# Output projection and second LayerNorm of an attention chunk ranked above older feed-forward work, in a one-core transformer block

## The chip, the cores and the metric

The kernel runs on one core of one Trainium2 chip. The metric is device time in microseconds (us), lower is better. A profile of one execution comes with each kernel; its span, from first to last instruction, is about 2 us shorter than the device time. Engines are named as the profile names them: PE is TensorE (matmul), PEld its weight loads, ACT is ScalarE, DVE is VectorE, POOL is GpSimd, SP issues the DMAs. L1039 is line 1039 of the kernel. Matmuls overlap in the records, so the cost of a matmul in a row is taken from the distance of their starts, not from the mean duration of one.

## The reference

A pre-LayerNorm transformer block: 2048 tokens, width 640, 32 heads of 20 columns, gated feed-forward (GLU) of width 1728, bf16.

```python
h  = x + attention(layernorm(x)) @ wo            # softmax over 2048 keys, 32 heads
hn = layernorm(h)                                # "LN2"
g  = hn @ w_gate ; u = hn @ w_up                 # 640 -> 1728
out = h + (gelu(g) * u) @ w_down                 # 1728 -> 640
```

## The kernel before

The queries are cut into seven chunks, numbered 0 to 6. The softmax needs 2048 x 2048 exps per head; ACT computes most of them, DVE eight tiles per slot (two in the first) with a polynomial; a slot is one chunk with a group of its heads. While ACT works on one chunk, PE fills the time between score and attention matmuls with work of earlier chunks: output projection, LN2, gate, up and down projection.

No engine program is written by hand. Every operation is recorded with a priority, and a list scheduler in the kernel's Python picks, for each engine, the ready operation with the lowest priority number, and the lowest recording number among equals (on PE an operation of the kind that ran last may go first). Its result is a fixed order of instructions per engine, with semaphore waits between them.

```python
SIZES = (512, 512, 256, 256, 256, 128, 128)
D_PER_SLOT = (8, 8, 8, 8, 8, 8, 8)               # exp tiles on DVE in each slot, per chunk
P_QK, P_PV, P_PRO, P_EPI, P_BG = 0, 1, 1.5, 2, 3
```

Two parts of one function record what follows the attention of a chunk. `tail` is true for chunk 6 only.

```python
def post(c, banks, tail):                        # cut
    p = P_EPI if tail else P_BG
    for tt in range(tb, tb + nt):
        # transpose of the attention output: by DMA, in the tail by PE and an ACT copy
        for hf in range(2):                      # output projection, 5 matmuls per half (L616)
            list(chain(bk, key, 320, [...wo...], [("hnT", tt), "wo"], p))
            op("dve", ...h_sb += bank..., p, ..., rel=[bk])                     # L1007
        ln_stats(h_sb[:, tt, :], t, ..., p)
    ln_rsqrt(q0 // 128, nt, p, table=tail)       # in the tail: Sqrt on ACT
    # normalize, transpose ...
    p = P_BG
    for k in range(nb):                          # gate (L1039), copied out by DVE (L1074)
        bg, kg = mms(k, wg, "wg", ...)
        cp.append(op("dve", ...tensor_copy..., p, ...))
    gl.append(op("act", ...Gelu..., -1, mode="gelu", ..., after=cp))
    for k in range(nb):                          # up (L1039), multiply by DVE (L1085)
        bu, ku = mms(k, wu, "wu", ...)
        hdone.append(op("dve", ...ALU.mult..., p, ...))
    # down (L1096), residual add (L1100), output DMA
```

A gelu needs another activation table than exp, so a gelu block in the exp phase has a table load before and one after it (1.28 us each in the traces). The scheduler also puts in filler matmuls, which compute nothing, where PE would otherwise have too little to do.

## Time and profile before

| | |
|---|---|
| device time, three runs | median 928.82 us (928.81 to 929.91) |
| span of the profiled run | 927.4 us |
| first steady exp, near 92 us, to the end of the last exp | 92.91 to 890.21: 797.3 us |
| the tail: end of the last exp to the end of the span | 37.2 us |

I call the second line the exp phase. It starts at the exp that waits 0.57 us for PE near 92 us.

From the page: part 1 (busy time, share of the span, instructions), and the shares by engine of the chain of work that ended last.

```profile
PE 837.1 (90%) x10069; PEld 356.9 (38%) x10126; DVE 811.3 (87%) x1703; ACT 883.2 (95%) x799; POOL 39.1 (4%) x117
ACT 73%; PE 14%; DVE 9%; DMA 2%; POOL 1%; issue 1%; SPq 0%
```

ACT sets the pace for most of the span. The tail is different. The timeline of ACT from 886 us (start, duration, what; in brackets how long ACT was idle before, and what ended it):

```profile
888.62 1.59 ACT L339 ACTIVATE rege<-ps 128x1536 bf16<-128x1536 f32 x1
890.23 1.28 ACT L339 ACT_TABLE_LOAD   x1
...
896.02 0.70 ACT L567 ACTIVATE rege<-ps 128x640 bf16<-128x640 bf16 x1 [4.29 <-PE ps L561]
901.39 0.21 ACT L339 ACTIVATE sd<-sd 128x1 bf16<-128x1 bf16 x1 [4.67 <-DVE sd L339]
901.61 1.28 ACT L339 ACT_TABLE_LOAD   x1
...
903.60 0.70 ACT L567 ACTIVATE rege<-ps 128x640 bf16<-128x640 bf16 x1 [0.49 <-PE ps L561]
904.20 1.69 ACT L339 ACTIVATE rege<-rege 128x1792 bf16<-128x1792 bf16 x1
```

These are: the last exp, the load for Sqrt, the copy of the last attention transpose, the Sqrt of the last LN2, the load for gelu, the copy of the last LN2's transpose, and last the gelu of chunk 5. The timeline of PE, without the small attention matmuls:

```profile
888.39 3.57 PE L1096 MATMUL ps<-regw,rege 128*128 128x320 bf16 x25
...
896.90 1.52 PE L616 MATMUL ps<-wo,rege 128*128 128x320 bf16 x10
898.26 0.98 PE L1096 MATMUL ps<-regw,rege 128*128 128x320 bf16 x6
899.08 4.21 PE L1039 MATMUL ps<-rege,regw 128*128 128x128 bf16 x70
903.12 0.44 PE L561 MATMUL ps<-ident,xn_t 128*128 128x128 bf16 x5
904.36 6.54 PE L1039 MATMUL ps<-rege,regw 128*128 128x128 bf16 x114 [0.80 <-ACT rege L567]
...
920.58 3.98 PE L1096 MATMUL ps<-regw,rege 128*128 128x320 bf16 x28 [0.52 <-DVE rege L1064]
```

PE hardly rests: it is idle 0.80 us before the 114 matmuls and 0.52 us before the last down projection. What it works on, above all, is the down projection of chunk 4 and the whole GLU of chunk 5, left over from the exp phase.

### The profile page before, as it was taken

Reading aid. Unit: us, or ns where it says so; the run is one execution under the profiler, and the core shown is the slowest. Engines: PE = TensorE matmul, PEld = TensorE weight load, DVE = VectorE, ACT = ScalarE, POOL = GpSimd, SP = SyncE. Lnnn points to the kernel's source line nnn. Section 1 sums busy time; section 2 is a strip of 40 time slices with the busy share of each in tenths; the row PEclk is TensorE's granted clock in tenths of the full one; section 3 lists DMA queues with packets and bytes.
Section 4 is the critical chain, followed back from the end, with each engine's and each line's share of the span. In section 5 each row is a group of like instructions: output and inputs, shape, how many; then the busy total and the mean of one; then the engine's idle time right before and its main releaser. Section 6 shows DMA issues by size and latency. Waiting matters only on the chain.

```text
span 927.4 us, 23141 instructions
## 1 busy us (share of the span) xinstructions
PE 837.1 (90%) x10069; PEld 356.9 (38%) x10126; DVE 811.3 (87%) x1703; ACT 883.2 (95%) x799; POOL 39.1 (4%) x117
## 2 busy tenths in 40 slices
PE   3998999899998998998797898999899998989998
PEld 2432322222232222233233333344345455546677
DVE  8859999999898998888798997988998997899972
ACT  6899999999999999999999999999999999999951
POOL 5000000000001000000001000000200200010100
PEclk9999999999999999999999999999999999999999
DMA  7301010322540000001021000011000100101000
GB/s 256 94 19 43 18 55 18 90 60 66 155 176 18 12 1 1 1 15 44 1 31 23 8 2 1 16 30 31 16 16 2 23 23 2 31 17 24 3 24 16
DMA packets 39517, 34.36 MB, mean 37 GB/s; under 512 B 19436, under 2 KB 36936, under 8 KB 39416
## 3 DMA queue, kind: packets, MB, share of 16 engines
q1 hardware_dynamic: 39416, 32.89, 12.7%
q8 instruction: 79, 1.29, 0.6%
q14 instruction: 22, 0.18, 0.1%
HBM read 20.12 MB, written 8.09 MB: 30 GB/s over the span
## 4 chain that ended last, share of the span: by engine, by line
ACT 73%; PE 14%; DVE 9%; DMA 2%; POOL 1%; issue 1%; SPq 0%
ACT pts L339 46%; ACT rege L339 25%; PE ps L1039 3%; PE ps L616 3%; DVE qt_all L339 3%; PE ps L1096 3%; PE ps L852 3%; PE ps L339 2%; DVE rege L339 2%; DMA regw<-in_A_wqkv_dram 1%; ACT L339 1%; DVE rege L812 1%; DVE qt_all L812 1%; POOL nw L339 0%; PE ps L561 0%
## 5 line engine op out<-in xcount | busy, mean ns | idle before, releaser
L339 ACT ACTIVATE pts<-ps 128x1536 bf16<-128x1536 f32 x480 | 571.7, 1368 | 5.1 <-PE ps L852 3.8
L852 PE MATMUL ps<-qt_all,kt_all 32*128 32x256 bf16 (+2 forms) x3584 | 304.9, 289 | 51.2 <-ACT pts L339 29.1
L339 ACT ACTIVATE rege<-ps 128x1536 bf16<-128x1536 f32 x239 | 298.8, 1367 | 2.4 <-PE ps L339 1.5
L852 PEld LDWEIGHTS ps<-qt_all,kt_all 32*128 32x128 bf16 x3584 | 96.4, 92 | 279.8 <-ACT pts L339 160.0
L339 DVE TENSOR_TENSOR qt_all<-qt_all 128x1024 bf16<-128x1024 bf16 (+1 forms) x240 | 164.4, 685 | 3.7
L1039 PE MATMUL ps<-rege,regw 128*128 128x256 bf16 (+2 forms) x957 | 149.2, 287 | 10.3 <-ACT rege L339 2.8
L339 PE MATMUL ps<-pts,v_all 128*21 128x256 bf16 (+2 forms) x2098 | 138.8, 290 | 1.0 <-DVE rege L339 1.0
L812 DVE TENSOR_SCALAR rege<-ps 128x512 int16<-128x512 f32 x154 | 105.3, 684 | 23.9 <-PE ps L852 23.1
L339 DVE TENSOR_SCALAR qt_all<-qt_all 128x1024 bf16<-128x1024 int16 (+1 forms) x288 | 115.8, 417 | 2.4
L339 PE MATMUL ps<-rege,v_all 128*21 128x256 bf16 (+2 forms) x1294 | 113.3, 292 | 0.1
L1039 PEld LDWEIGHTS ps<-rege,regw 128*128 128x128 bf16 x980 | 72.0, 97 | 65.4 <-issue 27.3
L616 PE MATMUL ps<-regw 128*128 128x512 bf16 (+1 forms) x342 | 82.1, 349 | 3.8 <-issue 1.3
L1096 PE MATMUL ps<-regw,rege 128*128 128x320 bf16 x448 | 78.7, 301 | 1.1 <-DVE rege L1064 0.5
L812 DVE TENSOR_SCALAR qt_all<-ps 128x512 int16<-128x512 f32 x96 | 65.6, 684 | 4.5 <-PE ps L852 3.6
L339 DVE TENSOR_SCALAR rege<-rege 128x1024 int16<-128x1024 int16 (+2 forms) x166 | 67.2, 421 | 1.3
L339 DVE TENSOR_TENSOR rege<-rege 128x1024 bf16<-128x1024 bf16 (+3 forms) x103 | 65.5, 644 | 0.9
L339 PEld LDWEIGHTS ps<-pts,v_all 128*21 128x21 bf16 x2098 | 50.2, 91 | 37.9 <-issue 31.7
L339 PE MATMUL ps<-kt_all,zer 128*32 128x512 bf16 x680 | 56.4, 384 | 0.0
L1085 DVE TENSOR_TENSOR rege<-rege,ps 128x512 bf16<-128x512 bf16 (+1 forms) x53 | 35.8, 677 | 16.4 <-PE ps L1039 16.4
L1096 PEld LDWEIGHTS ps<-regw,rege 128*128 128x128 bf16 x448 | 37.0, 97 | 32.7 <-issue 15.6
L339 PEld LDWEIGHTS ps<-rege,v_all 128*21 128x21 bf16 x1294 | 41.0, 91 | 20.6 <-issue 13.6
L616 PEld LDWEIGHTS ps<-regw 128*128 128x128 bf16 x360 | 28.6, 98 | 45.3 <-issue 20.9
(95 smaller groups left out, 575.3 us busy)
## 6 DMA issues: line engine op xcount, KB each, us to landing
rege<-in_A_x_dram SPq DMA_DIRECT2D x6, 640.0 KB, 5.2
q_rows<-regw SPq DMA_DIRECT2D x20, 128.0 KB, 1.7
out_dram<-rege SPq DMA_DIRECT2D x16, 160.0 KB, 2.0
regw<-in_B_w_gate_dram SPq DMA_DIRECT2D x1, 2160.0 KB, 13.3
regw<-in_B_w_up_dram SPq DMA_DIRECT2D x1, 2160.0 KB, 18.3
regw<-in_B_w_down_dram SPq DMA_DIRECT2D x1, 2080.0 KB, 23.4
kt_all<-k_rows SPq DMA_DIRECT2D x12, 160.0 KB
qt_all<-q_rows SPq DMA_DIRECT2D x12, 160.0 KB
```

The source lines that it names most:

```text
L339: return lambda eng: getattr(eng, method)(*args, **kwargs)
L616: yield op("pe", lambda eng, l=l, r=r, k=k: eng.matmul(bank(bk, n), l, r, start=(k == 0), stop=(k == len(steps) - 1)), c_mm(n), prio, mode ...
L812: d_ops.append(op("dve", lambda eng: eng.tensor_scalar(v[:, 512 * h:512 * h + 512], bank(b), EXP_MUL, -32000.0, ALU.mult, ALU.max), c_dve( ...
L852: return lambda eng: eng.matmul(out()[:, kk * nq:(kk + 1) * nq], kt_all[32 * j:32 * j + 32, g, kt * 128:(kt + 1) * 128], qt_all[32 * j:32 ...
L1039: op("pe", lambda eng, a=a, f=f, fi=fi: eng.matmul(bank(bk)[:, fi * nq:(fi + 1) * nq], w[:, a, F0[f]:F0[f] + 128], hnT[:, a, 128 * tb:128 ...
L1085: hdone.append(op("dve", lambda eng, bu=bu, fv=fv, w=w: eng.tensor_tensor(fv, fv, bank(bu, w), ALU.mult), c_dve(w), p, reads=[ku] + hkeys( ...
L1096: op("pe", lambda eng, f=f, o=o, hf=hf, bk=bk: eng.matmul(bank(bk, 320), ha_f[:, o:o + 128], wd[:, f, hf * 320:(hf + 1) * 320], start=(f = ...
```

## The change

The intent: a chunk's output projection and LN2 should not queue behind the older GLU matmuls, so that its own GLU can start earlier.

```diff
-D_PER_SLOT = (8, 8, 8, 8, 8, 8, 8)
+D_PER_SLOT = (8,) * len(SIZES)
-P_QK, P_PV, P_PRO, P_EPI, P_BG = 0, 1, 1.5, 2, 3
+P_QK, P_PV, P_PRO, P_EPI, P_LN, P_BG = 0, 1, 1.5, 2, 2.5, 3
@@ def post
-            p = P_EPI if tail else P_BG
+            p = P_EPI if tail else P_LN
-                                   for a in range(NA)], [("hnT", tt), "wo"], p))
+                                   for a in range(NA)], [("hnT", tt), "wo"], p, after=(sc.lw[("h", tt, hf)],)))
```

The first pair is the same tuple: there are seven sizes. The last line makes the output projection wait for the load of the chunk's residual input.

## The prediction

> **What bounds the kernel.** ScalarE, for most of the span: the page gives ACT 883.2 us busy (95%), and busy time by stretches 98 to 100% from 100 to 890 us. The chain of waits is 73% ACT. From 100 to 890 us ACT waits under 3 us in all. PE is near its limit too (95% from 700 to 800 us). After the last exp (890.2 us) the limit changes: the chain of the last 37 us is mostly PE (down projection L1096, gate/up L1039), with PE idle only 0.8 us at 904.4 and 0.5 us at 920.6.
>
> **What the change does.** The tuple for VectorE exp tiles has seven eights, as before: no change, and instruction totals confirm it. What is left is priority: output projection and LN2 ahead of older GLU work. Everything else is only moved, except 17 fewer filler matmuls (13 full, 4 narrow) and two more ACT table loads.
>
> **The exp phase.** ACT's work before the last exp is unchanged; the gelu blocks of three chunks move 8 to 12 exps earlier. I expect 0 +- 1 us. PE takes the earlier work in place of fillers and idle.
>
> **The tail, from the instruction order.** Now 53 down matmuls of chunk 4 follow the last score matmul; then 24 do. The 29 are worth 29 x 0.136 us (28 take 3.80 us) = 3.9 us of PE work. But chunk 5's gelu then stands between the last attention transpose copy and the Sqrt of the last LN2, with two added loads (1.28 us each). The trace shows 1.30 us from load to next activation; the Trainium skill, "ScalarE: Activation LUTs", section "What ACT_TABLE_LOAD costs", has about 2.66 us with a drain, which this trace does not show. Estimate: the gelu load hides in a wait; gelu starts at about 901.3, when the last gate copy is done; 1.69 us, load 1.28, Sqrt at 904.3 instead of 901.4. PE has no chunk work from about 899.8 to 903.0 (eight fillers and a wait), some 3.2 us. Then chunk 5's up matmuls cover the later LN2: its transposes come at about 905.9 instead of 903.1. At 0.057 us for a 128-column matmul the last up matmul ends at about 919.2 instead of 920.1.
>
> So 3.9 us less PE work, about 3 us more waiting: net -0.9 us. **Predicted 928.0 us** (before 928.82), range 925.8 to 930.3. Chances: faster by over 2% 0.01, within 2% 0.97, slower by over 2% 0.02. Two per cent is 18.6 us, half of the tail.
>
> **What would show it.** Right: the last exp ends at 890 +- 1, ACT over 99% busy to there; in the tail two more table loads around a 1.7 us gelu, the Sqrt about 3 us later, about 3 us of fillers and idle on PE before chunk 5's first up matmul. Wrong: ACT idle well over 3 us between 100 and 890 us; a PE stall on the chunk's residual input, for which the added dependency makes the output projection wait; the end over 2 us earlier, which would mean that the PE wait was smaller than I count.
>
> **What would make it wrong.** PE matmuls run in program order. Moved GLU matmuls that wait for a late VectorE copy (VectorE 88% busy) would hold back score matmuls and starve ACT; each such stall is tenths of a us, so dozens are needed for 2%. Fewer fillers might lower the granted clock; it is 1.0 almost throughout and I expect no change.

## The result

Time after: 927.52 us median of 4 runs (927.23 to 927.85); before, in the same rounds, 929.37 (928.81 to 931.93). The ratio of the fast runs is 0.9975, with a 95% interval of 0.9955 to 0.9994: a little faster. All ratios here are the mean time of one kernel's fast runs over that of the other's of the same rounds, so not quite the ratio of the medians quoted. A repetition later (e10) gave 0.9966 (0.9953 to 0.9980).

The two profiled spans are 927.4 and 925.5 us. They split into three parts:

| us | before | after | difference |
|---|---|---|---|
| up to the first steady exp | 92.91 | 92.84 | -0.07 |
| exp phase | 797.30 | 796.56 | -0.74 |
| tail | 37.19 | 36.10 | -1.09 |

The tail repeats within 0.1 us in every later profile of the two kernels, but the exp phase of the kernel before does not: two later looks at it (e11 and e12) took 798.06 and 798.05 us, while the changed kernel took 796.52 us again (e10). So the exp phase gains 0.7 us against this profile and 1.5 us against the other two. Two waits of ACT in this profile of the kernel before, and one that only the other two looks have (this is e12's), are absent after the change:

```profile
671.25 2.37 ACT L339 ACTIVATE pts<-ps 128x1536 bf16<-128x1536 f32 x2 [0.17 <-PE ps L852]
...
728.76 1.02 ACT L339 ACTIVATE rege<-ps 128x1024 bf16<-128x1024 f32 x1 [0.32 <-PE ps L852]
```

```profile
673.85 2.36 ACT L339 ACTIVATE rege<-ps 128x1536 bf16<-128x1536 f32 x2 [0.33 <-PE ps L852]
```

The same lines of the page, after:

```profile
PE 845.3 (91%) x10109; PEld 354.8 (38%) x10109; DVE 810.3 (88%) x1703; ACT 885.7 (96%) x801; POOL 35.1 (4%) x117
ACT 72%; PE 14%; DVE 11%; issue 1%; POOL 0%; DMA 0%
```

PE's busy time rises by 8.2 us although the program has 17 matmuls fewer. The count of records also rose, by 40, so part of this is only records that were missing in the first trace. The Trainium skill warns of this number in "Trainium Kernel Development and Optimization", section "Performance Expectations": matmul busy time is a bad metric for how close a kernel is to roofline, because matmuls are pipelined. Here it would mislead as a measure of work as well: it rises while the span falls.

ACT in the tail, after, from the last exp on:

```profile
887.77 1.63 ACT L339 ACTIVATE rege<-ps 128x1536 bf16<-128x1536 f32 x1
889.42 1.28 ACT L339 ACT_TABLE_LOAD   x1
...
895.62 0.70 ACT L567 ACTIVATE rege<-ps 128x640 bf16<-128x640 bf16 x1 [4.71 <-PE ps L561]
896.35 1.28 ACT L339 ACT_TABLE_LOAD   x1
900.49 1.70 ACT L339 ACTIVATE rege<-rege 128x1792 bf16<-128x1792 bf16 x1 [2.86 <-DVE rege L1074]
902.21 1.28 ACT L339 ACT_TABLE_LOAD   x1
903.50 0.21 ACT L339 ACTIVATE sd<-sd 128x1 bf16<-128x1 bf16 x1
903.72 1.28 ACT L339 ACT_TABLE_LOAD   x1
...
905.52 0.70 ACT L567 ACTIVATE rege<-ps 128x640 bf16<-128x640 bf16 x1 [0.30 <-PE ps L561]
```

The gelu of chunk 5 (900.49) now stands before the Sqrt (903.50), with a load on each side. PE in the tail, after:

```profile
887.57 3.43 PE L1096 MATMUL ps<-regw,rege 128*128 128x320 bf16 x24
...
896.49 1.52 PE L616 MATMUL ps<-wo,rege 128*128 128x320 bf16 x10
897.85 1.45 PE L1039 MATMUL ps<-rege,regw 128*128 128x128 bf16 x23
900.51 1.90 PE L339 MATMUL ps<-kt_all 128*128 128x512 bf16 x8 [1.21 <-DVE rege L1074]
902.25 2.96 PE L1039 MATMUL ps<-rege,regw 128*128 128x128 bf16 x50
905.04 0.44 PE L561 MATMUL ps<-ident,xn_t 128*128 128x128 bf16 x5
905.32 2.06 PE L1039 MATMUL ps<-rege,regw 128*128 128x128 bf16 x34
...
918.74 3.98 PE L1096 MATMUL ps<-regw,rege 128*128 128x320 bf16 x28 [0.52 <-DVE rege L1064]
```

Before, 53 down matmuls (L1096) of chunk 4 ran after the last score matmul; now 24 do. The 29 that went are worth 29 x 0.136 = 3.9 us. But between the end of the gate matmuls (897.85 + 1.45 = 899.30) and the first up matmul (902.25) PE has 2.95 us without work: 1.21 us idle and eight fillers. So most of the gain was given back. Adding up: -3.94 (down matmuls), +2.95 (this hole), -0.80 (the old wait before the 114, gone), +0.85 (two new waits for gate copies, 0.34 us at 894.02 and 0.51 us at 896.09) is -0.94; measured -1.09, so 0.15 us stays unassigned.

### The profile page after: what moved, and what is told of

Its sections match the earlier page's. It is cut to its first block, busy times and chain, and to the rows that moved or that the text cites. A ratio compares the mean times of both kernels' runs of the same rounds, so it can differ in the third digit from the quotient of the medians.

```text
span 925.5 us, 23154 instructions
## 1 busy us (share of the span) xinstructions
PE 845.3 (91%) x10109; PEld 354.8 (38%) x10109; DVE 810.3 (88%) x1703; ACT 885.7 (96%) x801; POOL 35.1 (4%) x117
## 3 DMA queue, kind: packets, MB, share of 16 engines
q8 instruction: 79, 1.29, 0.6%
## 4 chain that ended last, share of the span: by engine, by line
ACT 72%; PE 14%; DVE 11%; issue 1%; POOL 0%; DMA 0%
ACT pts L339 46%; ACT rege L339 25%; PE ps L1039 4%; DVE qt_all L339 3%; PE ps L616 3%; PE ps L852 3%; PE ps L339 3%; DVE rege L339 2%; PE ps L1096 2%; DVE qt_all L812 1%; DVE rege L812 1%; DVE stats L339 1%; ACT L339 1%; DVE rege L1074 1%; PE ps L561 0%
## 5 line engine op out<-in xcount | busy, mean ns | idle before, releaser
L1039 PE MATMUL ps<-rege,regw 128*128 128x256 bf16 (+2 forms) x980 | 154.7, 290 | 9.9 <-ACT rege L339 4.2
L616 PE MATMUL ps<-regw 128*128 128x512 bf16 (+1 forms) x360 | 86.9, 351 | 1.9 <-DVE v_all L749 0.7
L1096 PE MATMUL ps<-regw,rege 128*128 128x320 bf16 x448 | 79.4, 301 | 1.1 <-DVE rege L1064 0.5
L339 PEld LDWEIGHTS ps<-pts,v_all 128*21 128x21 bf16 x2098 | 50.2, 91 | 37.2 <-issue 31.6
L1096 PEld LDWEIGHTS ps<-regw,rege 128*128 128x128 bf16 x448 | 36.7, 97 | 32.4 <-issue 15.8
```

The lines of the kernel that those rows point to most:

```text
L339: return lambda eng: getattr(eng, method)(*args, **kwargs)
L616: yield op("pe", lambda eng, l=l, r=r, k=k: eng.matmul(bank(bk, n), l, r, start=(k == 0), stop=(k == len(steps) - 1)), c_mm(n), prio, mode ...
L1039: op("pe", lambda eng, a=a, f=f, fi=fi: eng.matmul(bank(bk)[:, fi * nq:(fi + 1) * nq], w[:, a, F0[f]:F0[f] + 128], hnT[:, a, 128 * tb:128 ...
L1096: op("pe", lambda eng, f=f, o=o, hf=hf, bk=bk: eng.matmul(bank(bk, 320), ha_f[:, o:o + 128], wd[:, f, hf * 320:(hf + 1) * 320], start=(f = ...
```

## The experiments

**Two theories without a run.** The change has two active parts, the rank and the added wait. The wait alone compiles to the same program as before, instruction by instruction on all five engines. The rank alone cannot be scheduled: the Python scheduler stops with "no operation can start". An argued reason, not traced further: without the wait, output projections take the PSUM banks before their residual input is there, and the operations that would bring it need those banks. So the wait alone costs nothing, and the rank cannot be scheduled without it. No profile shows PE waiting for the residual input.

Theory A, for the tail: the gain is the moved down matmuls less a new hole. The only PE work that could cover the last LN2 is chunk 5's up projection, which needs chunk 5's gelu, which needs all its gate matmuls, and these are no longer early enough. Rivals: B, only the amount of PE work left after the last score matmul counts; C, what the tail loses are the two added table loads before the Sqrt; D, the gain is made in the exp phase.

All kernels below are the changed kernel with the edit shown. All gave correct results. Spans are of the profiled run, unless said otherwise; the profiles other than e1's are at a mean granted clock of 0.998 or 1.

### e1 and e8: chunk 5's gelu after the last LN2

```diff
 # chunk 5's gelu waits for the second table load of the last LN2
+for x in held: sc.ops[x].deps.add(sc.lw["warmge"])
```

> The changed kernel, with chunk 5's gelu held until the last LN2's Sqrt and its gelu table load are done (14 table loads again, as before; the loads no longer stand between the last transpose copy and the Sqrt). Theory A (chunk 5's gelu is the input of the only PE work that can cover the last LN2): PE's wait of 3.1 us is not removed but becomes one of about 3.9 us in front of chunk 6's gate matmuls; profiled span about 0.7 us above the changed kernel's 925.5, so 925.8 to 926.8. Rival C (the added loads before the Sqrt are what the tail lost): two loads, 2.6 us, come back: span 922.5 to 923.5. Rival B (only PE work left after the last score matmul counts, and it is the same, 80 down and 280 gate/up): 925.5 +- 0.3.

> A second look at e1, whose profile fell in a slow state (its runs at full clock had spans of 925.5 to 926.5). Theory A: chunk 5's gelu after the last LN2's second table load; PE without chunk work for about 3.9 us between the end of chunk 5's gate matmuls and the first of the next 114, partly filled by six fillers; tail from the last exp's end about 36.8 us. Rival C (the two loads before the Sqrt are what is lost): tail 33.5 us.

The profile of e1 fell in a slow run: span 950.3 us at a clock of 0.854 throughout, so it is not used. Its four runs at full clock had spans of 925.5 to 926.5, 926.1 in the mean (a fifth, at 0.998, had 927.8), against 925.2 to 926.0 (925.6) for the changed kernel, which ran in other rounds. The ratio to before was 0.9985 (0.9971 to 0.9999). The second look, e8: span 926.2, tail 36.7 us. PE:

```profile
897.93 1.45 PE L1043 MATMUL ps<-rege,regw 128*128 128x128 bf16 x23
...
901.90 0.44 PE L561 MATMUL ps<-ident,xn_t 128*128 128x128 bf16 x5
903.21 6.54 PE L1043 MATMUL ps<-rege,regw 128*128 128x128 bf16 x114 [0.87 <-ACT rege L567]
```

The Sqrt came at 900.84, 2.7 us earlier, and two loads were gone, yet the tail grew by 0.6 us: from 899.38 to 903.21 PE had only fillers and five transposes. Rival C falls: the two loads were hidden. In the changed kernel the first (896.35) ran in a wait of ACT, the other (902.21) while PE had the 50 up matmuls. Theory A's 0.7 us is met; B's "no difference" is missed by 0.6 us.

### e2: the new rank for chunk 4 alone

```diff
-p = P_EPI if tail else P_LN
+p = P_EPI if tail else P_LN if c == 4 else P_BG
```

> The changed kernel with the new rank for chunk 4 alone. By instruction order 60 down matmuls and 280 gate/up follow the last score matmul (changed kernel: 80 and 280; before: 109 and 280), 50 of chunk 5's gate matmuls stand before the last attention matmuls, and chunk 5's gelu comes before the last transpose copy. Theory A: PE has work until the last LN2 is done; tail from the last exp's end to the end of the span about 31.7 us (changed kernel 36.1), span 920.5 to 923. Rival B (PE work left): 24.0 us of matmuls left against 26.7, so 2.7 us less: span about 922.8. Rival D (the gain lies in the exp phase of chunks 1 to 3, which lose their rank here): the last exp ends about 0.8 us later, at 890.2, and the span is at or above 925.5.

Median 926.34 us, ratio 0.9968 (0.9953 to 0.9982); span 923.9 (expected 920.5 to 923), tail 32.1 us, within 0.4 us of theory A. But the exp phase took 799.6 us, 3.1 us longer than the changed kernel's. One wait of ACT, absent in both kernels, is half of it:

```profile
811.98 4.62 ACT L339 ACTIVATE pts<-ps 128x1536 bf16<-128x1536 f32 x4 [1.58 <-PE ps L339]
```

Another 0.8 us are waits at 671, 673 and 729 us, as in the looks at the kernel before. So the tail gains 4.0 us and the exp phase gives 3.1 back. Rival D is right in part: the exp phase depends on which chunks have the rank, by several times the 0.8 us that I allowed.

### e3: chunk 5's gate before chunk 4's down projection

```diff
-bg, kg = mms(k, wg, "wg", ...)
+bg, kg = mms(k, wg, "wg", ..., P_LN if c == len(CHUNKS) - 2 else P_BG)
+for x in held: sc.ops[x].deps.add(exp_ops[-1])      # its gelu right after the last exp
```

> The changed kernel with chunk 5's gate matmuls ranked with LN2, so they run before chunk 4's down matmuls, and chunk 5's gelu held to just after the last exp (15 table loads). After the last score matmul 112 down matmuls and 210 up/gate are left (27.8 us by 0.136 and 0.0565 us each), more than the changed kernel's 26.7. Theory A: gelu no longer waits for gate matmuls in the tail, down matmuls cover the attention epilogue and the LN2: PE waits under 1 us in all before the last down matmuls; tail about 34.2 us, span 922.8 to 924.5. Rival B (PE work left decides): 1.1 us above the changed kernel, about 926.6.

This run separates A from B, as it leaves PE more work in the tail. Median 926.18 us, ratio 0.9961 (0.9948 to 0.9975); span 923.7, tail 34.9 us (expected 34.2), exp phase 796.6. ACT, then PE:

```profile
887.32 1.48 ACT L339 ACTIVATE rege<-ps 128x1536 bf16<-128x1536 f32 x1
888.88 1.28 ACT L339 ACT_TABLE_LOAD   x1
890.18 1.70 ACT L339 ACTIVATE rege<-rege 128x1792 bf16<-128x1792 bf16 x1
```

```profile
898.42 2.20 PE L1103 MATMUL ps<-regw,rege 128*128 128x320 bf16 x15
900.46 2.96 PE L1043 MATMUL ps<-rege,regw 128*128 128x128 bf16 x50
903.25 0.44 PE L561 MATMUL ps<-ident,xn_t 128*128 128x128 bf16 x5
```

The gelu is done 10.3 us earlier, while ACT has nothing else to do; the down matmuls need no gelu of chunk 5 and fill the time of the last LN2; the hole is gone. PE had 1.1 us more work by count, and the tail is 1.2 us shorter than the changed kernel's. Rival B falls. The 0.7 us that the tail is over my number are waits that I did not count, 0.84 us before the 19 down matmuls after the last score matmul and 0.59 us at 895.01.

### e4: the new rank for chunks 1 to 3 alone

```diff
-p = P_EPI if tail else P_LN
+p = P_EPI if tail else P_LN if c < 4 else P_BG
```

> The changed kernel with the new rank for chunks 1, 2 and 3 alone; chunks 4 and 5 as before. After the last score matmul 98 down and 269 gate/up matmuls are left, 28.5 us. Theory A: chunk 5's gate ends later, its gelu starts about 0.8 us later after the last exp than in the changed kernel (11.1 us after it), tail about 36.8 us; the last exp ends where the changed kernel's does, 889.4; span about 926.2. Rival B (PE work left): 1.8 us more than the changed kernel, 927.3. Rival D (the gain is made in the exp phase, by the early chunks): last exp's end 889.4, span within 0.3 us of 925.5.

Median 930.39 us, ratio 1.0008 (0.9994 to 1.0023); span 928.7. The exp phase is 796.6 us, as in the changed kernel: the 0.7 to 1.5 us that the change gains there come with the rank of chunks 1 to 3, the part of rival D that holds. (The edit leaves chunk 0 its rank too; e9 below takes it away and has the same exp phase.) The tail is 39.1 us, 2.3 us above theory A. PE shows why:

```profile
901.71 0.39 PE L339 MATMUL ps<-kt_all 128*128 128x512 bf16 x1 [0.49 <-DVE rege L1074]
903.84 4.59 PE L1039 MATMUL ps<-rege,regw 128*128 128x128 bf16 x50 [1.74 <-ACT rege L339]
```

The 50 up matmuls took 4.59 us instead of the 2.96 us in the changed kernel, 1.6 of the 2.3 us. The granted clock (the column after POOL) in stretches of 2 us:

```profile
902.00:904.00 2.00, 0.26 (x4) 0.16 (x4) 0.35 (x4) 1.89 (x2) 0.00 (x0) 0.99 0.00 0
904.00:906.00 2.00, 2.00 (x22) 2.00 (x21) 0.00 (x0) 1.97 (x3) 0.00 (x0) 0.50 0.00 0
906.00:908.00 2.00, 2.00 (x27) 2.00 (x26) 1.29 (x4) 0.81 (x2) 0.00 (x0) 0.65 0.00 0
```

With one filler in the hole instead of eight, the clock fell to half: cut finer, it is 0.50 from 904.0 to 907.3 us and 1.00 from 907.5 on. That the missing fillers are the cause was a new theory, so I tested it.

### e5: no fillers in the tail

```diff
-self.order = order
+end = max(k for k, o in enumerate(order) if o.tag and o.tag[0] == "S")   # last score matmuls
+self.order = [o for k, o in enumerate(order) if not (k > end and o.tag == "warm")]
```

> The changed kernel without the eight filler matmuls after the last score matmul; nothing else moved. In the early-chunks run one filler stood in this place, and the granted clock fell to 0.50 and 0.65 in the two 2 us stretches after it, where 50 up matmuls took 4.59 us instead of 2.96. Theory F (the fillers hold the clock through the wait for chunk 5's gelu): the same fall here, the first 50 up matmuls take 4 us or more, span 927.2 to 928.2, mean clock 0.998. Rival (the fillers only occupy PE): the up matmuls start 0.1 to 0.2 us earlier, span 925.3.

Median 928.53 us, ratio 0.9984 (0.9971 to 0.9996); span 926.5, tail 37.8 us, 1.7 us longer than the changed kernel's.

```profile
901.58 4.59 PE L1040 MATMUL ps<-rege,regw 128*128 128x128 bf16 x50 [2.94 <-ACT rege L340]
```

```profile
902.00:904.00 2.00, 2.00 (x25) 2.00 (x23) 0.67 (x2) 1.97 (x3) 0.00 (x0) 0.57 0.00 0
904.00:906.00 2.00, 2.00 (x24) 2.00 (x22) 1.07 (x4) 0.54 (x2) 0.00 (x0) 0.58 0.00 0
```

Here it is 0.50 from 902.3 to 905.6 us. Three of the five runs had a mean clock of 0.998 (spans 926.5 to 927.5), two had 1.0 (925.8 both); the changed kernel had 1.0 in all nine of its runs. So the fillers do hold the clock in this place, but without them it seems to fall in some runs only (only one of the three was profiled), and my 927.2 to 928.2 was too high for the profiled one. Where it did not fall, leaving the fillers out cost nothing that I could tell.

### e6 and e7: both remedies together

The gate-first edit of e3, with the rank for chunk 4 (e6) or for chunks 3 and 4 (e7):

```diff
-p = P_EPI if tail else P_LN
+p = P_EPI if tail else P_LN if c in (3, 4) else P_BG     # e6: c == 4
```

> The gate-first kernel with the new rank for chunk 4 alone: all of chunk 5's gate matmuls before the last score matmul, 89 down and 210 up/gate after it (24.0 us of matmuls against 27.8 in the gate-first run), no fillers in the tail. Theory A: PE waits only for the last exp and for the last multiply; tail 30.4 us after the last exp's end (gate-first run 34.9). The exp phase should show the 1.6 us stall near 812 us and other small ones of the chunk-4-only run, so the last exp ends about 3 us later after the same start of the exps; span about 921 to 922.5. Rival B (PE work left in the tail alone, exp phase as in the gate-first run): 3.8 us less than that run, 919.9.

> As e6, with the new rank for chunks 3 and 4. The order of the tail is that of e6, number by number; chunk 3's work runs at other places in the exp phase (chunk 2's gelu 13 exps later). Theory A: tail 30.4 us, as e6; the difference between the two lies in the exp phase alone, where I expect less than 1 us; span 921 to 922.5.

e6: median 926.55 us, ratio 0.9965 (0.9952 to 0.9977), span 924.5 (expected 921 to 922.5), exp phase 799.7, tail 31.6. e7: median 924.73 us, ratio 0.9940 (0.9926 to 0.9953), span 922.0, exp phase 798.2, tail 31.6. The tails are equal, as their orders are; both are 1.2 us over the 30.4 us. A part of that is a wait that I had not counted, 1.05 us for the multiply of chunk 5's up projection:

```profile
899.53 2.08 PE L1043 MATMUL ps<-rege,regw 128*128 128x128 bf16 x32
902.66 1.80 PE L1103 MATMUL ps<-regw,rege 128*128 128x320 bf16 x12 [1.05 <-DVE rege L1092]
```

The exp phases differ by 1.5 us where I expected under 1: the 1.58 us wait near 812 us is in e6, as in e2, and not in e7. e7 beats both kernels and has the lowest median of all that I ran, though its interval overlaps that of e9, and at the edge those of e3 and e6. Two of e6's runs had a clock of 0.998 with no PE wait over 1.1 us in its profiled tail, so such a clock does not by itself point to a hole there.

### e9 and e10: the exp phase of the change with a tail of the gate-first kind

e9 is e7 with the rank for chunks 1 to 4; e10 is the changed kernel, unedited, on the same chip in the same rounds.

> As e7, with the new rank for chunks 1 to 4. It should join the exp phase of the changed kernel (from the exp after 0.57 us of waiting near 92 us to the last exp's end: changed kernel 796.6 us, e7 798.2, before 797.3) to a tail with chunk 5's gate done early. By instruction order 112 down and 210 up/gate matmuls follow the last score matmul, 36 of the down matmuls before the last attention matmuls, which start some 1.3 us later than in e7 for it. If the two parts add: exp phase 796.6 +- 0.3, tail about 32.6 us (e7 31.6), span about 921.4 from an exp start at 92.2. If the last down matmuls ahead of the attention cost more than I count, the tail is 34 us or more and e7 stays the fastest.

> The changed kernel once more, beside the same runs of the kernel before as e9: ratio 0.9975 to 0.999; span of full-clock runs 925.0 to 926.5; exp phase 796.6 +- 0.2, tail 36.1 +- 0.2.

e9: median 925.48 us, ratio 0.9946 (0.9932 to 0.9960), span 923.3, exp phase 796.6, tail 33.4 (expected 32.6). e10: median 927.77 us, ratio 0.9966 (0.9953 to 0.9980), span 925.4, exp phase 796.5, tail 36.2. The exp phase met the number, the tail was 0.8 us over, so the parts add up: 93.3 + 796.6 + 33.4 = 923.3 (the span expected was 921.4, from an exp start at 92.2). The ratio of e10 lies below the 0.9975 to 0.999 that I expected: seven of the nine runs of the kernel before in these rounds had a clock of 0.998. Two of e9's runs had a clock of 0.998 and spans of 925.0 and 925.3; all five of e10 had 1.0.

### e11 and e12: the kernel before, twice more

Of the 29 runs of the kernel before that went with e1 to e10, 17 had a mean clock of 1.0 (mean span 927.5 us), 11 of 0.998 (929.4) and one of 0.995 (932.0). The changed kernel had 1.0 in all nine. So a part of the measured ratio may be that the kernel before loses its clock somewhere.

> The kernel before, profiled again. Of its 29 runs so far beside the others 17 had a mean granted clock of 1.0 (mean span 927.5 us), 11 of 0.998 (929.4) and one of 0.995 (932.0); the changed kernel had 1.0 in all of 9. If this look falls in the 0.998 group, the stretch where the clock is below 1.0 should lie in the tail, after PE's longest idle there (0.8 us near 904 us plus fillers missing), and the tail should be some 1.9 us above 37.2 us. If the dip lies elsewhere (at the start, or in the exp phase), the changed kernel's immunity has nothing to do with its tail. If it falls at 1.0, the question stays open.

> As e11, a second look, to raise the chance that one falls in the 0.998 group.

Both fell at 1.0, with spans of 928.5 and 927.9. Where the kernel before loses clock in its other runs is open. As an estimate, one stretch of 3.4 us at half clock, as in e4 and e5, costs 1.7 us and brings the mean over 926 us to 0.998, so one such fall would account for the 1.9 us between the two groups; no profile caught it. At clock 1.0, the mean spans are 927.5 us (17 runs) before and 925.7 us (9 runs) after: 1.8 us, close to the 1.9 us of the two profiles, so the split above does not rest on those runs. But the spans of both looks are longer than the first profile's, mostly by their exp phases (798.06 and 798.05 us); their tails are the same 37.2 us.

## Why the prediction was right

- **Time.** Predicted 928.0 us, range 925.8 to 930.3; measured 927.52. Two per cent were out of reach, as said. The gain itself was mis-sized: 0.9 us was forecast, and the medians of the same rounds differ by 1.85 us, the two profiles by 1.9. The tail gave about what was forecast; the rest came from the exp phase, where I had put zero. So that the time fell so near is in part luck.
- **ACT bounds the kernel up to the last exp, PE after it.** Right. Part by part, ACT is 99.9% busy from 600 to 800 us after the change, and the tail is PE with few gaps.
- **The tuple changes nothing.** Right: as many exp tiles on ACT and DVE.
- **Exp phase 0 +- 1 us.** Measured -0.74 us, within it but not zero, and -1.5 us against the looks e11 and e12, which is outside it. e4 shows that it comes with the rank of chunks 1 to 3. ACT's waits at 671 us (0.17 us) and 729 us (0.32 us) are gone after the change; they are two thirds of the 0.74. The third wait, near 674 us in e11 (0.42 us) and e12 (0.33 us), is about half of what these two take longer; what decides whether it comes is open. I wrote that three gelu blocks move "8 to 12 exps earlier"; the instruction order has 10, 6 and 13.
- **29 down matmuls leave the tail, 3.9 us.** Right by count and by the distance of starts.
- **About 3 us of new waiting on PE.** Predicted 3.2 us from 899.8 to 903.0; measured 2.95 us from 899.3 to 902.25. Counted from the end of the last exp (890.2 us in the prediction, 889.40 after the change), the gelu was predicted at +11.1 and came at +11.1 us, the Sqrt at +14.1 and came at +14.1, the last up matmul was to end at +29.0 and ended at about +28.8. The net of the tail was -0.9 us by prediction, -1.09 measured.
- **The table load costs 1.30 us.** Right. After the gelu ends (902.19) the load starts at 902.21 and the Sqrt at 903.50.
- **What I did not see.** I took the loads before the Sqrt as a loss beside the hole; e8 shows that removing them gains nothing while the hole is there. I counted the eight fillers as lost time only; e4 and e5 show that they keep the clock up. And I did not ask whether the kernel before had all its clock: 12 of its 29 runs later did not.

Where the gain went, in one sentence: the new rank let 3.9 us of down projection run earlier, but chunk 5's gate still came last, and everything that PE had left needed its gelu or the last LN2, so PE met a hole of 2.95 us; running that gate first (e3) closes it.

## What to carry to other kernels

When priorities move work out of a tail, ask next what each remaining piece waits for: an amount of work is only worth its time if some of it can run in each wait. Work without open dependencies (here an older chunk's down projection) is best kept for the latency chain at the end, and work that feeds another engine (here the gate before a gelu) is best done first. Count from one fixed event, here the end of the last exp, to compare tails: the start of the kernel alone moves by 1 us from run to run.

## What the Trainium skill lacked or had wrong

- "ScalarE: Activation LUTs", section "What ACT_TABLE_LOAD costs": about 1283 ns for the load agrees (1.28 us here), the further drain of about 1.38 us for each switch is not to be seen: from the start of the load to the next activation are 1.29 to 1.30 us where that one is ready, and in the exp phase and the tail of both kernels the load starts 0.02 us after the activation before it.
- "TensorE: Matmul & The Clock Gate", section "HAM oscillation — how this bites in real kernels", warns of PE-idle gaps above about 3.4 us. Here the clock fell to 0.50 after shorter ones: after a gap of 2.94 us (e5, whose mean clock was 0.998 in three of five runs), and after two gaps of 0.49 and 1.74 us with one filler of 0.39 us between them (e4, mean clock 0.998 in all five).
- No page that I read has a granted clock of 0.854 in a program on a single core; one run of e1 had it throughout, with a span of 950.3 us instead of 926. Nothing here shows its cause.
